# Reordering the first loads and spreading the recurrence's VectorE steps in a kernel that mixes an FFT filter with a state-space recurrence

## The chip, the cores and the metric

The kernel runs on one core of a Trainium2 chip. The metric is the device time of one execution in microseconds (us). Each experiment was timed several times, beside runs of the kernel before on the same chip. A run is called slow when it is over 1.5% above the fastest run of the same kernel; ratios use fast runs only.

Engines: PE is TensorE (matmul; its weight loads are listed as PEld), DVE is VectorE, ACT is ScalarE, POOL is GpSimd, SP is SyncE, which here only issues DMAs. In these traces an instruction that waits holds up those behind it on its engine.

## The reference

With x of 2048 x 1024 in bf16, the output is `g*a + (1-g)*b`:

```python
g = sigmoid((x * gate_w).sum(-1, keepdims=True))
a = irfft2(rfft2(x) * (w_r + 1j*w_i), s=(2048, 1024))     # over both axes
# b: a diagonal complex recurrence over the 2048 rows
Bu = einsum("bld,pd->blp", x, B_bar)
h[t] = Lam_bar * h[t-1] + Bu[t]
b = 2 * einsum("blp,dp->bld", h, Cmat).real + x * Dskip
```

## The kernel before: the parts that matter

The work has three parts.

- **Start**: eight x tiles are loaded, and `fstage` transforms each of them along the rows (product `ps_f` on TensorE).
- **FFT part**: 16 groups `g` run through `fd` (product `ps_d` with the table `G`), `bf_w` (products with `MM`, then VectorE multiplies by the filter `W` into `Y`) and `bi` (`ps_q`); then the inverse transform (`ps_id`, `ps_y`) writes `a` to a scratch in DRAM.
- **Last part**: the gates, then 16 output tiles (product `psy`).

The recurrence runs beside the FFT and the last part. It comes in 16 pairs (4 chunks of rows times 4 pairs of state blocks). A pair is 32 matmuls `psu` of `xT` (x transposed by DMA) with `BT`, four evictions by ScalarE into `u`, and ten large VectorE steps:

```python
def ssm_pair(c, q):
    u = up.tile([P, 2, 2, TC], BF16, name="u", tag="u")
    for jj in range(2):
        for ri in range(2):
            ...                                  # 8 matmuls psu <- BT, xT
            nc.scalar.activation(out=u[:, jj, ri, :], in_=psu, func=ACT.Copy, scale=...)
            if not (jj and ri):
                yield 1.8
    nc.vector.tensor_mul(out=cu, in0=u, in1=...)           # 3 products and sums
    ...
    nc.vector.tensor_tensor_scan(out=su[:, jj, ri, :], ...) # 4 scans
    ...
    nc.vector.tensor_add(out=h, in0=cu, in1=u)             # 3 products and sums
    yield 1.8
```

A `yield` only tells the program, while it is being written out, how much work the generator has emitted; a loop uses it to interleave the recurrence with the FFT. SP and POOL keep the program's order; a scheduler orders the other engines.

The loads of the start:

```python
xts = [load_x(jj) for jj in range(8)]                 # SP's queue
...
for jj in range(8):
    for _ in fstage(jj): pass
    if jj == 5:
        start_consts()      # G_sb, FI_sb    on POOL's queue
        load_M(0)           # MM             on POOL's queue
        load_W(0)           # W              on POOL's queue
    if jj == 4:
        nc.gpsimd.tensor_copy(out=BT[:, 0, 0, 0, 0:1], in_=xts[6][:, 0, 0:1])   # holds BT(0) back until x tile 6 is in
        load_BT(0); load_xT(0); load_BT(1); load_BT(2); load_BT(3)              # transposing DMAs, SP's queue
load_M(1); load_W(1); load_M(2)                       # POOL's queue
```

Of the kernel before, what the change touches and what calls it, by code (L numbers as in the profile page):

```python
# [10 lines left out]
ACT = mybir.ActivationFunctionType  # L11
ALU = mybir.AluOpType
FP32 = mybir.dt.float32
BF16 = mybir.dt.bfloat16
# [6 lines left out]
D = 1024  # L21
K = 512
P = 128
TC = 512
# [101 lines left out]
GN = 2308  # L126
# [10 lines left out]
def kernel(  # L137
# [17 lines left out]
    nc = tc.nc  # L155
# [54 lines left out]
        for ri, src in enumerate((B_B_re, B_B_im)):  # L210
            nc.sync.dma_start_transpose(out=BT[:, jb, ri], in_=src[P * jb:P * (jb + 1), :])

    def load_xT(c):
        for h in range(2):
            r0 = TC * c + 256 * h
            nc.sync.dma_start_transpose(out=xT[:, :, r0:r0 + 256], in_=x[r0:r0 + 256, :])

    xts = [load_x(jj) for jj in range(8)]

    vps = psU.tile([P, 4, 8], BF16, name="vps", tag="psu")  # L220
    for i in range(4):
# [117 lines left out]
        a, s = 4 * (q % 2), TC * (q // 2)  # L339
        return xT[:, a:a + 4, s:s + TC].rearrange("p (j r) t -> p j r t", r=2)  # L340

    def ssm_pair(c, q):
        u = up.tile([P, 2, 2, TC], BF16, name="u", tag="u")
        for jj in range(2):
            jb = 2 * q + jj
            for ri in range(2):
                psu = psU.tile([P, TC], FP32, name="psu", tag="psu")
                for dblk in range(8):
                    nc.tensor.matmul(psu, lhsT=BT[:, jb, ri, dblk, :], rhs=xT[:, dblk, TC * c:TC * (c + 1)],  # L349
                                     start=(dblk == 0), stop=(dblk == 7))  # L350
                nc.scalar.activation(out=u[:, jj, ri, :], in_=psu, func=ACT.Copy,  # L351
                                     scale=(nrho if ri else rho)[:, jb:jb + 1])
                if not (jj and ri):
                    yield 1.8
        tq = tab[:, 2 * q:2 * q + 2]
        full = [P, 2, 2, TC]
        cu = rp.tile(full, BF16, name="cu", tag="cu")
        su = rp.tile(full, BF16, name="su", tag="su")
        nc.vector.tensor_mul(out=cu, in0=u, in1=tq[:, :, 0:1, :].to_broadcast(full))  # L359
        nc.vector.tensor_mul(out=su, in0=u[:, :, ::-1, :], in1=tq[:, :, 1:3, :])  # L360
        nc.vector.tensor_add(out=cu, in0=cu, in1=su)  # L361
        for jj in range(2):
            jb = 2 * q + jj
            for ri in range(2):
                nc.vector.tensor_tensor_scan(out=su[:, jj, ri, :], data0=r_sb[:, jb:jb + 1].to_broadcast([P, TC]),  # L365
                                             data1=cu[:, jj, ri, :],
                                             initial=(0.0 if c == 0 else carry[q][:, jj, ri:ri + 1]),
                                             op0=ALU.mult, op1=ALU.add)
        if c + 1 < NCH:
            ge = su[:, :, :, TC - 1]  # L370
            k1 = sm.tile([P, 2, 2], FP32, name="k1")
            nc.vector.tensor_mul(out=k1, in0=ge, in1=cTC[:, 2 * q:2 * q + 2].unsqueeze(2).to_broadcast([P, 2, 2]))
            k2 = sm.tile([P, 2, 2], FP32, name="k2")
            nc.vector.tensor_mul(out=k2, in0=ge[:, :, ::-1], in1=sg[:, 2 * q:2 * q + 2, :])
            cy = sm.tile([P, 2, 2], FP32, name=f"carry{q}")
            nc.vector.tensor_add(out=cy, in0=k1, in1=k2)
            carry[q] = cy
        h = h_tile(c, q)
        nc.vector.tensor_mul(out=cu, in0=su, in1=tq[:, :, 0:1, ::-1].to_broadcast(full))  # L379
        nc.vector.tensor_mul(out=u, in0=su[:, :, ::-1, :], in1=tq[:, :, 1:3, ::-1])  # L380
        nc.vector.tensor_add(out=h, in0=cu, in1=u)
        hs[c, q] = h
        yield 1.8


    eos = {}
# [1 line left out]
    def fstage(jj):  # L388
# [15 lines left out]
        for eo_i in range(2):  # L404
            for b in range(2):
# [9 lines left out]
                (nc.vector.tensor_copy if eo_i else nc.scalar.copy)(  # L415
                    out=FX[:, q + 1, :, j0:j0 + 4], in_=ps[:, :, 1, :].rearrange("p j c -> p c j"))
                yield 1.0

    gctx = ExitStack()
    gc1 = gctx.enter_context(tc.tile_pool(name="gc1", bufs=1))  # L420
    fr = gctx.enter_context(tc.tile_pool(name="fr", bufs=2))
    G_sb = gc1.tile([P, GN], BF16, name="G_sb")
    FI_sb = fc.tile([P, 2 * P], BF16, name="FI_sb")

    def start_consts():
        nc.gpsimd.dma_start(out=G_sb, in_=cG)
        nc.gpsimd.dma_start(out=FI_sb, in_=cFI)

    MM = {}
    WT = {}  # L430
    Wtiles = [gc1.tile([P, 2, 514], BF16, name=f"W{i}") for i in range(2)]
    for w in Wtiles:
        nc.gpsimd.memset(w[:, :, 513:514], 0.0)
    Xtiles = [gc1.tile([P, 2, 514], BF16, name=f"X{i}") for i in range(2)]
    for w in Xtiles:
        nc.gpsimd.memset(w[:, :, 513:514], 0.0)

    def load_M(g):
        m = fr.tile([P, 6, P], BF16, name="MM", bufs=3)
        (nc.gpsimd if g < 3 else nc.sync).dma_start(out=m, in_=cMM[g])  # L440
        MM[g] = m

    def load_W(g):
        w = Wtiles[g % 2]
        for ri, src in enumerate((A_w_r, A_w_i)):
            rows = bass.AP(src.tensor, src.offset + g * 513, [[32 * 513, 64], [((32 - 2 * g) if g else 16) * 513, 2], [1, 513]])
            nc.gpsimd.dma_start(out=w[:, ri, 0:513], in_=rows)
        WT[g] = w

    X1s, Ys = {}, {}  # L450
    Gi_sb = None
# [147 lines left out]
    def load_C(half):  # L599
# [7 lines left out]

    sp_work = {
        0: [lambda: load_BT(4)], 1: [lambda: load_BT(5)], 2: [lambda: load_BT(6)], 3: [lambda: load_BT(7)],
        5: [lambda: load_xT(1)], 7: [lambda: load_xT(2)], 9: [lambda: load_xT(3)], 11: [lambda: load_C(0)],  # L610
    }

    for jj in range(8):
        for _ in fstage(jj):
            pass
        if jj == 5:
            start_consts()
            load_M(0)
            load_W(0)
        if jj == 4:  # L620
            nc.gpsimd.tensor_copy(out=BT[:, 0, 0, 0, 0:1], in_=xts[6][:, 0, 0:1])
            load_BT(0)
            load_xT(0)
            load_BT(1)
            load_BT(2)
            load_BT(3)
    load_M(1)
    load_W(1)
    load_M(2)

    def ssm_all():
        for c in range(NCH):
            for q in range(4):
                if c == 0:
                    tables(q)
                yield from ssm_pair(c, q)

    class Gen:
        def __init__(self, g):
# [15 lines left out]
    ssm = Gen(ssm_all())  # L655
    fft = Gen(fft_main())
    while not fft.done:
        if ssm.t < 28.8 * (fft.t - 3.5) / (84 - 3.5) and ssm.t < 28.0:
            ssm.step()
        else:  # L660
            fft.step()
    while ssm.t < 28.0:
        ssm.step()
    load_C(1)
    order1.close()
# [2 lines left out]
    with ExitStack() as bctx:  # L668
# [3 lines left out]
        dsk_bc = fin1.tile([P, D], BF16, name="dsk_bc")  # L672
        nc.gpsimd.dma_start(out=dsk_bc, in_=B_Dskip.partition_broadcast(P))

        lrow = fin1.tile([1, 2, D], BF16, name="lrow")
        pc = psY.tile([P, 16], FP32, name="pc", tag="psy")
        gf = fin1.tile([P, 16], FP32, name="gf")
        om = fin1.tile([P, 16], FP32, name="om")

        def gates():  # L680
            for hf in range(2):
                pg = psY.tile([P, D], FP32, name="pg", tag="psy")
                for ch in range(2):
                    t0 = TC * (2 * hf + ch)
                    for dblk in range(8):
                        nc.tensor.matmul(pg[0:1, TC * ch:TC * (ch + 1)], lhsT=gwT[:, dblk:dblk + 1],
                                         rhs=xT[:, dblk, t0:t0 + TC], start=(dblk == 0), stop=(dblk == 7))
                nc.scalar.copy(out=lrow[:, 0, :], in_=pg[0:1, :])
                nc.vector.tensor_sub(out=lrow[:, 1, :], in0=pg[0:1, :], in1=lrow[:, 0, :])
                for tb in range(8):  # L690
                    for i in range(2):
                        nc.tensor.matmul(pc[:, 8 * hf + tb:8 * hf + tb + 1], lhsT=lrow[:, i, P * tb:P * (tb + 1)],
                                         rhs=one, start=(i == 0), stop=(i == 1))
            gb = fin1.tile([P, 16], BF16, name="gb")
            nc.scalar.activation(out=gb, in_=pc, func=ACT.Sigmoid)
            nc.vector.tensor_copy(out=gf, in_=gb)
# [4 lines left out]
        fins = {}  # L701

        def tile_in(tb):
            xc = fin.tile([P, D], BF16, name="xc", bufs=4)
            gac = fin.tile([P, D], BF16, name="gac", bufs=4)
            nc.sync.dma_start(out=xc, in_=x[P * tb:P * (tb + 1), :])
            nc.sync.dma_start(out=gac, in_=ya_dram[P * tb:P * (tb + 1), :])
            nc.vector.tensor_mul(out=xc, in0=xc, in1=dsk_bc)
            nc.scalar.activation(out=gac, in_=gac, func=ACT.Copy, scale=gf[:, tb:tb + 1])  # L709
            fins[tb] = xc, gac  # L710

        psys = {}
# [21 lines left out]
                nc.sync.dma_start(out=out2[P * tb:P * (tb + 1), ds], in_=o[:, ds])  # L734

        def c_all():
            for tb, dh in ((0, 0), (1, 0), (2, 0), (0, 1), (1, 1), (2, 1)):
                if tb + 2 < 5 and dh == 0:
                    tile_in(tb + 1)
                half(tb, dh)  # L740
                yield 3.6
            for tb in range(3, 16):
                if tb + 1 < 16:
                    tile_in(tb + 1)
                half(tb, 0)
                yield 3.6
                half(tb, 1)
                yield 3.6

        while ssm.t < 28.8 + 14.0:  # L750
            ssm.step()
        gates()
        tile_in(0)
        cg = Gen(c_all())
        t0 = ssm.t
        while not cg.done:
# [34 lines left out]
```

## Time and profile before

Time before the change: 387.31 us, median of 3 runs (385.66 to 396.58). The profiled run took 398.2 us (span 396.4 us) and is slow, so it is some 3% longer than the two fast ones (385.66 and 387.31 us).

The first fence holds three rows of the page's busy table of before. Each digit is a fortieth of the span (9.9 us) in tenths of busy time; PEclk is the clock granted to TensorE, in tenths.

```profile
PE   3840889969699598899979999999999999999995
...
DVE  4930345895787499952997799999999999997121
...
PEclk9995799989879899999989999999999999999999
```

Slice 4 (29.7 to 39.6 us) has a 0 for TensorE, and so it has for VectorE. From slice 22 on TensorE is full to the end.

What was waited for, from the waits view of before (engine, line, what ended the wait: total us, times, longest):

```profile
PE psu L349 <- DMA xT<-in_A_x_dram: 17.3, 1, 17.3
...
PE ps_xe L481 <- DMA MM<-c_MM: 8.5, 2, 4.7
...
PE pc L692 <- DVE lrow L689: 2.2, 1, 2.2
```

TensorE waits 17.3 us in one piece for `xT`, 8.5 us for `MM`, and once 2.2 us for the gates' rows (`lrow`). Why is `xT` late? Its two transposing DMAs are issued from 17.6 us on, and the last of them lands at 41.1 us. The next two fences are DMA views of before by queue (q1 is SP's queue, q0 POOL's): first 18 to 38 us, when the copies of POOL's queue (`G`, `FI`, three `MM`, two `W`: 1.7 MB) are in flight, then 41 to 46 us, when they are through.

```profile
q1 hardware_dynamic: 4477, 1.13, 65.4%
q0 software_dynamic: 499, 1.61, 46.0%
```

```profile
q1 hardware_dynamic: 4122, 1.02, 103.8%
```

In the first stretch the transposes move 1.13 MB in 20 us (57 GB/s); in the second 1.02 MB in 5 us (205 GB/s). Their packets are small (1.02 MB in 4122 packets, 250 bytes each), those of the copies large (1.61 MB in 499, 3.2 KB each). The late `xT` moves everything: the first `ps_d` runs at 45.7 us, although the x tiles have landed by about 15. On TensorE the first `psu` runs ahead of the last x tile's `ps_f` and ahead of `ps_d`. From TensorE's timeline of before (start us, us, engine, line, what; in brackets the idle time and what ended it):

```profile
41.24 1.44 PE L349 MATMUL psu<-xT,BT 128*128 128x512 bf16 x3 [17.34 <-DMA xT<-in_A_x_dram]
42.48 0.42 PE L410 MATMUL ps_f<-BT,eo 128*128 128x256 bf16 x1
...
45.66 0.82 PE L458 MATMUL ps_d<-G_sb,big 128*128 128x512 bf16 x5
```

### The profile page before, as it was taken

Reading aid. Unit: us, or ns where it says so; the run is one execution under the profiler, and the core shown is the slowest. Engines: PE = TensorE matmul, PEld = TensorE weight load, DVE = VectorE, ACT = ScalarE, POOL = GpSimd, SP = SyncE. Lnnn points to the kernel's source line nnn. Section 1 sums busy time; section 2 is a strip of 40 time slices with the busy share of each in tenths; the row PEclk is TensorE's granted clock in tenths of the full one; section 3 lists DMA queues with packets and bytes.
Section 4 is the critical chain, followed back from the end, with each engine's and each line's share of the span. In section 5 each row is a group of like instructions: output and inputs, shape, how many; then the busy total and the mean of one; then the engine's idle time right before and its main releaser. Section 6 shows DMA issues by size and latency. Waiting matters only on the chain.

```text
span 396.4 us, 4950 instructions
## 1 busy us (share of the span) xinstructions
PE 346.6 (87%) x1860; PEld 180.9 (46%) x1860; DVE 292.7 (74%) x408; ACT 182.9 (46%) x252; POOL 32.3 (8%) x83
## 2 busy tenths in 40 slices
PE   3840889969699598899979999999999999999995
PEld 2630556635465265564324444444444444444442
DVE  4930345895787499952997799999999999997121
ACT  2960399939677587986325231412322232211100
POOL 4550012202211000000000000000000000000000
PEclk9995799989879899999989999999999999999999
DMA  7799939765969511327950023221121022034001
GB/s 270 233 182 90 166 85 203 209 129 130 179 158 163 122 60 73 141 107 184 187 186 1 2 79 82 78 79 26 55 79 54 27 79 80 2 96 140 30 26 54
DMA packets 65064, 42.91 MB, mean 108 GB/s; under 512 B 52400, under 2 KB 54448, under 8 KB 65040
## 3 DMA queue, kind: packets, MB, share of 16 engines
q1 hardware_dynamic: 62560, 36.12, 38.6%
q0 software_dynamic: 2128, 6.30, 7.0%
q8 instruction: 14, 0.23, 0.3%
q10 hardware_dynamic: 352, 0.17, 0.1%
q14 instruction: 10, 0.08, 0.1%
HBM read 21.61 MB, written 8.39 MB: 76 GB/s over the span
## 4 chain that ended last, share of the span: by engine, by line
PE 58%; DVE 18%; DMA 10%; ACT 7%; SPq 3%; issue 2%; DVEq 0%; POOL 0%; ACTq 0%; POOLq 0%
PE psy L723 28%; PE psu L349 20%; DMA xT<-in_A_x_dram 5%; DVE su L365 5%; DMA xt<-in_A_x_dram 3%; DMA MM<-c_MM 3%; PE ps_d L458 2%; PE psy L726 2%; SPq L603 1%; DVE su L360 1%; DVE cu L379 1%; ACT X L470 1%; DVE cu L359 1%; DVE u L380 1%; ACT X L491 1%
## 5 line engine op out<-in xcount | busy, mean ns | idle before, releaser
L349 PE MATMUL psu<-xT,BT 128*128 128x512 bf16 x512 | 121.5, 383 | 17.4 <-DMA xT<-in_A_x_dram 17.3
L349 PEld LDWEIGHTS <-BT 128*128 128x128 bf16 x512 | 49.7, 98 | 74.9 <-issue 20.4
L365 DVE TENSOR_TENSOR_SCAN su<-r_sb,carry,cu 128x512 bf16<-128x512 f32 x48 | 57.7, 1264 | 0.4
L351 ACT ACTIVATE u<-psu,nrho 128x512 bf16<-128x512 f32 x32 | 22.1, 690 | 60.1 <-PE psu L349 60.1
L723 PEld LDWEIGHTS <-h 128*128 128x128 bf16 x256 | 25.0, 98 | 30.2 <-issue 0.5
L709 ACT ACTIVATE gac<-gac,gf 128x1024 bf16<-128x1024 bf16 x16 | 18.1, 1146 | 39.0 <-DMA gac<-ya_scratch 36.0
L732 DVE SCALAR_TENSOR_TENSOR o<-psy,om,gac 128x1024 bf16<-128x1024 f32 (+1 forms) x17 | 20.6, 1215 | 21.0 <-PE psy L726 21.0
L351 ACT ACTIVATE u<-psu,rho 128x512 bf16<-128x512 f32 x32 | 22.0, 687 | 22.8 <-PE psu L349 22.6
L359 DVE TENSOR_TENSOR cu<-u,tab 128x2048 bf16<-128x2048 bf16 x16 | 19.5, 1219 | 15.3 <-ACT u L351 15.2
L495 DVE TENSOR_TENSOR Y<-X,W 128x1028 bf16<-128x1028 bf16 x16 | 11.1, 693 | 25.8 <-ACT X L491 25.8
L723 PE MATMUL psy<-CT,h 128*128 128x512 bf16 x128 | 29.3, 379 | 0.0
L723 PE MATMUL psy<-big,h 128*128 128x512 bf16 x128 | 28.9, 379 | 0.0
L516 PE MATMUL ps_q<-MM,Y 128*128 128x256 bf16 x64 | 17.2, 298 | 5.3 <-DVE Y L497 3.2
L415 DVE CAST big<-ps_f 128x512 bf16<-128x512 f32 x8 | 5.5, 683 | 21.5 <-ACT big L414 21.5
L458 PE MATMUL ps_d<-G_sb,big 128*128 128x256 bf16 (+3 forms) x128 | 20.5, 300 | 0.0
L379 DVE TENSOR_TENSOR cu<-su,tab 128x2048 bf16<-128x2048 bf16 x16 | 19.5, 1218 | 0.1
L361 DVE TENSOR_TENSOR cu<-cu,su 128x2048 bf16<-128x2048 bf16 x16 | 19.5, 1217 | 0.1
L360 DVE TENSOR_TENSOR su<-u,tab 128x2048 bf16<-128x2048 bf16 x16 | 19.5, 1217 | 0.0
L380 DVE TENSOR_TENSOR u<-su,tab 128x2048 bf16<-128x2048 bf16 x16 | 19.5, 1216 | 0.0
L723 PEld LDWEIGHTS <-xT 128*128 128x128 bf16 x128 | 12.5, 98 | 15.1
L723 PEld LDWEIGHTS <-big 128*128 128x128 bf16 x128 | 12.5, 98 | 15.1
L410 PE MATMUL ps_f<-BT,eo 128*128 128x256 bf16 x64 | 17.6, 311 | 1.7 <-DVE big L415 1.5
(170 smaller groups left out, 579.4 us busy)
## 6 DMA issues: line engine op xcount, KB each, us to landing
ya_scratch<-ya SPq DMA_DIRECT2D x16, 256.0 KB, 2.0
xc<-in_A_x_dram SPq DMA_DIRECT2D x16, 256.0 KB, 2.9
gac<-ya_scratch SPq DMA_DIRECT2D x16, 256.0 KB, 2.9
out_dram<-o SPq DMA_DIRECT2D x15, 256.0 KB, 2.0
MM<-c_MM SPq DMA_DIRECT2D x13, 192.0 KB, 2.6
W<-in_A_w_r_dram POOLq DMA_DIRECT2D x16, 128.2 KB, 4.2
W<-in_A_w_i_dram POOLq DMA_DIRECT2D x16, 128.2 KB, 3.7
xt<-in_A_x_dram SPq DMA_DIRECT2D x4, 512.0 KB, 4.3
```

The source lines that it names most:

```text
L349: nc.tensor.matmul(psu, lhsT=BT[:, jb, ri, dblk, :], rhs=xT[:, dblk, TC * c:TC * (c + 1)], start=(dblk == 0), stop=(dblk == 7))
L351: nc.scalar.activation(out=u[:, jj, ri, :], in_=psu, func=ACT.Copy, scale=(nrho if ri else rho)[:, jb:jb + 1])
L359: nc.vector.tensor_mul(out=cu, in0=u, in1=tq[:, :, 0:1, :].to_broadcast(full))
L360: nc.vector.tensor_mul(out=su, in0=u[:, :, ::-1, :], in1=tq[:, :, 1:3, :])
L361: nc.vector.tensor_add(out=cu, in0=cu, in1=su)
L365: nc.vector.tensor_tensor_scan(out=su[:, jj, ri, :], data0=r_sb[:, jb:jb + 1].to_broadcast([P, TC]), data1=cu[:, jj, ri, :], initial=(0.0 ...
L379: nc.vector.tensor_mul(out=cu, in0=su, in1=tq[:, :, 0:1, ::-1].to_broadcast(full))
L380: nc.vector.tensor_mul(out=u, in0=su[:, :, ::-1, :], in1=tq[:, :, 1:3, ::-1])
L458: nc.tensor.matmul(ps[:, lo:lo + w], lhsT=FX[:, q, 8 * g:8 * g + 8, :], rhs=G_sb[:, o:o + w], start=start, stop=stop, skip_group_check=True)
L709: nc.scalar.activation(out=gac, in_=gac, func=ACT.Copy, scale=gf[:, tb:tb + 1])
L723: nc.tensor.matmul(psy[:, ds], lhsT=hs[c, jb // 2][:, jb % 2, ri, P * tq:P * (tq + 1)], rhs=CT[dh][:, jb, ri, :], start=(i == 0), stop=False)
L732: nc.vector.scalar_tensor_tensor(out=o[:, ds], in0=psy[:, ds], scalar=om[:, tb:tb + 1], in1=gac[:, ds], op0=ALU.mult, op1=ALU.add)
```

## The change

Its intent: bring in everything that the first FFT groups need, then run the transposes with nothing beside them; break up the transposes inside the FFT; and emit the ten VectorE steps of a pair one at a time among the FFT's steps, so that no FFT step waits behind a whole pair. The diff, cut to its core:

```diff
-    xts = [load_x(jj) for jj in range(8)]
+    xts = [load_x(jj) for jj in range(5)]
+    nc.sync.dma_start(out=G_sb, in_=cG)
+    xts.append(load_x(5))
+    load_M(0)
+    xts.append(load_x(6))
+    load_W(0)
+    xts.append(load_x(7))
+    load_M(1); load_W(1); load_M(2)            # all on SP's queue now
+    nc.sync.dma_start(out=FI_sb, in_=cFI)
...                                             # and the BT(0) hold waits for x tile 7
-        5: [load_xT(1)], 7: [load_xT(2)], 9: [load_xT(3)], 11: [load_C(0)],
+        13: [load_C(0)],
+    for i in range(6):
+        sp_work[5 + i] = [load_xT(1 + i // 2, (i % 2,))]     # one half per group
...
-    def ssm_pair(c, q):           # TensorE, ScalarE and all VectorE steps
+    def ssm_pe(c, q, u):          # TensorE and ScalarE, a yield after each eviction
+    def ssm_dve(c, q, u):         # a yield after each of ten VectorE steps
...
+                for i, _ in enumerate(ssm_pe(c, q, u)):
+                    yield 0.5
+                    for _ in range(2 + i % 2):
+                        next(prev, None)         # steps of the pair before
+                        yield 0.52
+                prev = ssm_dve(c, q, u)
...
-        if ssm.t < 28.8 * (fft.t - 3.5) / (84 - 3.5) and ssm.t < 28.0:
+        if ssm.t < 28.8 * (fft.t - 3.5) / (88 - 3.5) and ssm.t < 30:
...
-        while ssm.t < 28.8 + 14.0:              # how far the recurrence is when the gates come
+        while ssm.t < 41:
...                                             # last part, in words:
-    gates(): row sums, their transposing products `pc`, sigmoid, all before the first output tile
+    gates(): row sums only;  gates2(): the rest, after the second half tile
+    scaling gac by the gate: ScalarE, just before a tile's second half
+    tiles are loaded two ahead instead of one
```

So the VectorE steps of a pair now stand beside the matmuls of the next pair, one pair later than before. No arithmetic is added or taken away.

## The prediction

> **What bounds the kernel now.** The profiled run (396.4 us, flagged slow; timed runs 385.7 to 396.6) has three parts.
>
> 1. *Start, to 45.7 us.* The timeline shows TensorE idle from 24.0 to 41.2 us; the waits view charges 17.3 us of it to the DMA of xT. Two transposing loads each of xT and BT (1.5 MB) are issued from 14.9 us; xT lands at 41.1. While POOL's copies (G, FI, three MM, two W: 1.7 MB) are in flight, the DMA view shows mostly 60 to 210 GB/s; after them the next transposes run at about 290. So the transposes are starved, which fits the Trainium skill ("DMA: Bandwidth & Descriptors", section "Queues, rings and completion order"): each DMA engine round-robins between queues packet by packet, and transposes have small packets. The first product of G (ps_d) runs only at 45.7 us, though the x tiles are in by about 15.
> 2. *FFT with four recurrence pairs, 45.7 to 183 us.* TensorE 87%, ScalarE 82%, VectorE 72% busy: none is the limit; in-order queues make them wait. The chain of waits shows 6.9 and 3.1 us for MM behind transposes in SP's queue, 5.9 us of SP issuing CT's transposes ahead of the last MM, and VectorE recurrence steps (four scans, 4.5 us) ahead of Y and pm.
> 3. *After that.* TensorE is 100% busy from 206 us on, VectorE 95% until 362. A pair takes 14.24 us of TensorE, about 13.7 of VectorE.
>
> **What the change does.**
> - Start: about 1 MB goes ahead of the last x tile: at 380 GB/s (seen there) +3 us on x, but only 0.7 MB, in the same queue, still competes with the transposes. Estimate: transposes from 18.5 us, xT landed by 28 to 30. G, MM and W are there when the last x tile is transformed (about 25 us), so ps_d starts at about 27, not 45.7.
> - FFT phase: xT in six single transposes, CT after the last MM: about -10 us of MM stalls. VectorE steps come one by one, about 3.2 instead of 4 pairs of them (11.9 us each) in this phase: -3 to -8 us. Phase about 124 instead of 137 us.
> - After: gates come after 5.7 pairs instead of 6, their transposing products later: -5 us before the first output tile, but +3 us of recurrence left, and VectorE one pair behind. From the FFT's end TensorE needs about 213 us, VectorE 210 (12.8 pairs, 12 tiles at 1.8, a 31 us tail): no gain; VectorE may become co-limiting.
>
> No arithmetic is added or removed.
>
> **Sum.** 27 + 124 + 213 = about 365 us. What start and FFT phase save is nearly all critical, since everything else comes after. What the slow flag means is unknown: if before's fast runs lost less in the start, the gain is smaller than against the profile. Predicted 365 us, 80% range 353 to 378. Faster by over 2%: 0.88; within 2%: 0.10; slower: 0.02.
>
> **What would show it.** First ps_d at 25 to 30 us; psu's wait for xT down from 17.3 to under 5 us; no 10 us gap with every engine idle; MM waits under 3 us in all; FFT end (last ps_y) near 150 us; from there about 213 us, TensorE full, VectorE over 95%.
>
> **What would make it wrong.** psu placed ahead of ps_d on TensorE, still waiting for xT; x tiles delayed by more than 3 us; W loads, still on POOL's queue, starving the later transposes; VectorE, a pair behind, costing the last part 5 to 15 us; the granted clock (0.5 in some stretches) moving.

## The result

The changed kernel took 370.1 us (median of 4 runs, 367.28 to 370.15). Before, with one more run, had 391.94 us (385.66 to 397.66). The ratio is 0.953 (95% interval 0.9445 to 0.9616); a ratio here is the mean time of one kernel's fast runs over that of the other's fast runs of the same rounds, so it is not quite the ratio of the medians. On another chip (the run changed_again) it was 0.9418. The change is faster by 4.7% and 5.8% on these two.

The same views of the changed kernel, profiled with a span of 368.3 us. The busy table, in slices of 9.2 us:

```profile
PE   3978899999987999999959999999999999999995
...
DVE  4958358997999643994987999999999999997221
...
PEclk9999999999998999999998999999999999999999
```

The hole at the start is gone. From the waits view:

```profile
ACT gac L757 <- DVE gf L713: 9.9, 1, 9.9
...
PE psu L382 <- ACT u L384: 5.0, 2, 4.7
DVE xc L725 <- DMA gac<-ya_scratch: 4.9, 1, 4.9
...
PE psu L382 <- DMA xT<-in_A_x_dram: 1.1, 1, 1.1
```

The wait for `xT` fell from 17.3 to 1.1 us, and no wait of TensorE for `MM` is left in the list. But there are new ones: ScalarE waits 9.9 us for `gf`, and TensorE 4.7 us in one piece for ScalarE. The DMA view of the changed kernel from 19 to 35 us, where the first transposes run, shows no packet of POOL's queue (q0); q1 moved its 2.91 MB at 182 GB/s:

```profile
q1 hardware_dynamic: 11530, 2.91, 107.3%
```

On TensorE `ps_d` now stands ahead of the first `psu`:

```profile
27.64 0.82 PE L469 MATMUL ps_d<-G_sb,big 128*128 128x512 bf16 x5
29.60 0.38 PE L382 MATMUL psu<-xT,BT 128*128 128x512 bf16 x1 [1.14 <-DMA xT<-in_A_x_dram]
```

Three marks in time, read from the timelines, divide the span (us; the third column is the changed kernel on the second chip):

| | before (slow run) | changed | changed_again |
|---|---|---|---|
| first `ps_d` | 45.7 | 27.6 | 27.7 |
| end of the last `ps_y` | 180.1 | 149.4 | 147.2 |
| FFT part, the difference | 134.4 | 121.8 | 119.5 |
| from there to the end of the span | 216.3 | 218.9 | 220.2 |

(The prediction put the end of before's FFT part at 183 us, where the loads of the last part begin; by the measure of this table it is 180.1.) The start gained 18 us, the FFT part 12.6, and the last part lost 2.6. Part of the difference to the slow run is its state.

**The clock is part of it.** The next fence shows the five stretches of before where TensorE had work at half clock. Columns: stretch, its us, busy us of PE, PEld, DVE, ACT and POOL with instruction counts, PEclk, DMA share, GB/s.

```profile
41.20:45.60 4.40, 4.36 (x19) 2.63 (x20) 0.56 (x1) 0.58 (x1) 0.00 (x0) 0.52 1.02 203
86.30:89.80 3.50, 3.49 (x16) 2.35 (x17) 3.50 (x5) 1.01 (x1) 0.57 (x1) 0.51 0.00 0
106.80:113.70 6.90, 5.88 (x24) 3.22 (x25) 6.39 (x11) 2.25 (x4) 1.71 (x3) 0.51 1.09 243
134.10:137.60 3.50, 3.50 (x18) 2.15 (x16) 1.01 (x2) 2.51 (x4) 0.00 (x0) 0.51 0.00 0
202.40:205.80 3.40, 3.40 (x11) 0.89 (x9) 3.40 (x4) 1.00 (x1) 0.00 (x0) 0.50 0.31 114
```

Together they last 21.7 us, so with the clock at half they cost at most half of that, 10.9 us (an estimate). They come just after TensorE stood still: for `xT` until 41.2, for `Y` until 86.3, for `MM` until 107.8 and 134.0, for the gates until 201.9. The Trainium skill has a rule for this ("TensorE: Matmul & The Clock Gate", Part 1, the clock gate): after an idle window of about 3.4 us the clock is halved, and a busy window of about 3.4 us brings it back. On the length of the slow stretches this trace agrees: four of them last about 3.4 or 6.9 us, and in the fifth only the end of a longer one had work. On the idle window it does not: the stalls before them lasted 17.3, 3.0, 3.7, 4.7 and 2.2 us, so that two were shorter than 3.4 us. The changed kernel has two stretches, both after a stall (the first after a wait of 2.6 us for the inverse table `Gi_sb`; the stall before the second is the middle line):

```profile
114.80:118.20 3.40, 3.40 (x17) 2.44 (x15) 2.70 (x3) 2.50 (x3) 0.00 (x0) 0.50 0.01 2
188.90:193.30 4.40, 0.33 (x2) 0.05 (x1) 3.44 (x7) 1.14 (x2) 0.00 (x0) 1.00 0.00 0
193.30:196.70 3.40, 2.77 (x7) 0.99 (x7) 1.17 (x2) 3.40 (x6) 0.00 (x0) 0.50 0.02 5
```

They last 6.8 us, at most 3.4 us lost. So up to some 7 of the 28 us between the two profiles (an estimate, the difference of these two) are clock that stalls no longer take away; they are part of the gains by stage above, not a further gain. The mean granted clock, 0.957 before, is 0.989 now. It also goes with the spread from run to run: of the 7 runs of before on one chip, the fastest (389.55 us) had 0.973 and the slowest (401.09 us) 0.950.

### The profile page after: what moved, and what is told of

The parts are those of the page before. It is cut to its first block, busy times and chain, and to the rows that moved or that the text cites. A ratio compares the mean times of both kernels' runs of the same rounds, so it can differ in the third digit from the quotient of the medians.

```text
span 368.3 us, 4955 instructions
## 1 busy us (share of the span) xinstructions
PE 340.3 (92%) x1860; PEld 178.9 (49%) x1860; DVE 294.0 (80%) x408; ACT 180.0 (49%) x252; POOL 28.3 (8%) x74
## 4 chain that ended last, share of the span: by engine, by line
PE 57%; issue 17%; DMA 9%; DVE 6%; POOL 5%; SPq 4%; ACT 0%; ACTq 0%; DVEq 0%; POOLq 0%
PE psy L739 27%; PE psu L382 20%; PE ps_id L538 5%; POOL W L239 4%; SPq L614 3%; DMA CT<-in_A_x_dram 2%; DMA W<-in_A_w_i_dram 2%; PE psy L742 2%; DMA Gi_sb<-c_Gi 1%; DVE su L402 1%; DMA vec<-in_B_Lambda_im_dram 1%; PE ps_y L560 1%; DMA gac<-ya_scratch 1%; PE ps_y L559 1%; PE ps_y L558 1%
## 5 line engine op out<-in xcount | busy, mean ns | idle before, releaser
L384 ACT ACTIVATE u<-psu,rho 128x512 bf16<-128x512 f32 x32 | 22.2, 695 | 41.7 <-PE psu L382 32.1
L384 ACT ACTIVATE u<-psu,nrho 128x512 bf16<-128x512 f32 x32 | 22.2, 692 | 14.5 <-PE psu L382 14.3
L538 PE MATMUL ps_id<-Gi_sb,big 128*128 128x256 bf16 (+3 forms) x128 | 18.8, 304 | 2.6 <-DMA Gi_sb<-c_Gi 2.6
L527 PE MATMUL ps_q<-MM,Y 128*128 128x256 bf16 x64 | 15.4, 274 | 5.4 <-DVE Y L508 2.8
L739 PEld LDWEIGHTS <-big 128*128 128x128 bf16 x128 | 12.5, 98 | 15.1
L739 PEld LDWEIGHTS <-xT 128*128 128x128 bf16 x128 | 12.5, 98 | 15.1
L452 PE MATMUL ps_f<-BT,eo 128*128 128x256 bf16 x64 | 16.8, 302 | 3.1 <-ACT big L457 1.7
L538 PEld LDWEIGHTS <-big 128*128 128x128 bf16 x128 | 15.9, 148 | 6.4 <-issue 3.3
```

Source lines behind the costliest of these rows:

```text
L538: nc.tensor.matmul(ps[:, lo:lo + w], lhsT=FX[:, q, :, j], rhs=Gi_sb[:, o:o + w], start=start, stop=stop, skip_group_check=True)
L739: nc.tensor.matmul(psy[:, ds], lhsT=hs[c, jb // 2][:, jb % 2, ri, P * tq:P * (tq + 1)], rhs=CT[dh][:, jb, ri, :], start=(i == 0), stop=False)
```

## The experiments

Theory 1: the start carries most of the gain, because the transposes are freed of the copies in the other queue. Theory 2: spreading the VectorE steps carries it. Twelve kernels ran; all gave correct results. Kernels are compared below by the means of their fast runs where they ran on one chip; where they did not, the text says so.

### One part alone, or all but one (one chip)

**start_only**: before, with only the new start.

```diff
 # before
+    G, MM(0), W(0) between the x tiles; MM(1), W(1), MM(2), FI behind them; SP's queue; BT(0) held for x tile 7
```

> The kernel before with only the start changed (tables, W and G between the x tiles on SP's queue, transposes after the last x tile). Theory 1 (the start carries most of the gain): first ps_d near 28 us instead of 45.7, xT wait of psu about 1 us, time 10 to 18 us under before, about 370 to 377 us. Theory 2 (the spread of VectorE's steps carries it): less than 6 us under before, because VectorE stays the limit later on.

Measured: 373.99 us, ratio 0.9539 (0.9468 to 0.9611). First `ps_d` at 28.4 us.

**no_start**: the changed kernel with before's start.

```diff
 # changed
-    G, MM, W, FI early on SP's queue
+    G, MM, W, FI after fstage(5) on POOL's queue; BT(0) held for x tile 6
```

> The changed kernel with the start put back as it was (tables on POOL's queue, beside the transposes). Theory 1: first ps_d back near 40 to 46 us, time 10 to 18 us above the changed kernel, about 380 to 388. Theory 2: under 376 us.

Measured: 382.01 us, ratio 0.9757 (0.9682 to 0.9831). First `ps_d` at 45.0 us, and `psu` waits 16.7 us for `xT`.

**spread_only**: before, with the new emission of VectorE's steps and its constants.

```diff
 # before
-    ssm_pair; 84, 28.0
+    ssm_pe and ssm_dve, one step at a time; 88, 30
```

> The kernel before with only the VectorE steps spread (and the mixing constants that go with it, gates where before has them). Theory 1: 0 to 6 us under before's fast runs, 381 to 388 us. Theory 2: 8 us or more under before, below 379.

Measured: 392.52 us, ratio 1.0032 (0.9952 to 1.0111): nothing (before itself took 392.55 us on this chip, more than the absolute numbers above assumed). In its profile (span 390.0 us) the FFT part takes 123.4 us (42.5 to 166.0), 11 less than in the slow profile of before, but 224.0 us remain after it, 8 more than in before. The reason stands in its waits view:

```profile
PE pc L709 <- DVE lrow L706: 8.4, 1, 8.4
```

VectorE, now a pair behind, makes `lrow` late, and the gates' products, still in their old place, hold TensorE for 8.4 us. The changed kernel moves them to a later place (`gates2`).

**no_spread**: the changed kernel with before's emission.

```diff
 # changed
-    ssm_pe and ssm_dve; 88, 30, 41
+    ssm_pair; 84, 28.0, 28.8 + 14.0
```

> The changed kernel with the recurrence's VectorE steps emitted pair by pair as before and before's mixing constants and gate position; start, SP order and end stay changed. Theory 1: within 6 us of the changed kernel, 367 to 376 us. Theory 2: 376 us or more.

Measured: 369.21 us, ratio 0.9425 (0.9362 to 0.9488). That is as fast as the changed kernel (0.953 and 0.9418 on two other chips).

What follows: theory 1 holds. The start alone gives 4.6%; without it 2.4% are left. The spread gives nothing measurable, neither alone nor as the last part added. But it is not idle: its FFT part ends at 149.4 us in the changed kernel and at 154.5 in no_spread, whose last part is shorter (212.9 us against 218.9). What the spread gains in the FFT part is lost afterwards. Where, the last two groups show.

### The order on SP's queue (second chip, with the next two)

**changed_again**: the changed kernel unaltered, for comparison.

> The changed kernel itself, for comparison on one chip. Both theories: 367 to 371 us, 0.94 to 0.955 of before.

Measured: 368.73 us, ratio 0.9418 (0.9287 to 0.9549).

**no_spwork**: the changed kernel with before's transposes inside the FFT.

```diff
 # changed
-    one half of xT at each of groups 5 to 10, CT at 13
+    a whole xT at groups 5, 7 and 9, CT at 11
```

> The changed kernel with the transposes inside the FFT put back (xT by pairs at four groups, CT ahead of the last MM). If the MM waits behind transposes cost what the chain of waits of before showed (some 10 us): 4 to 10 us above the changed kernel, MM waits of 5 us or more. If they only moved slack: within 2 us of it.

Measured: 374.31 us, ratio 0.9601 (0.9507 to 0.9695). The means of the fast runs are 374.1 against 367.7 us for changed_again: 6.4 us (5.3 if changed_again's run of 372.24 us, which counts as slow, is taken in). `MM` waits are back, 5.0 us of them in one piece:

```profile
PE ps_xe L492 <- DMA MM<-c_MM: 5.5, 2, 5.0
```

So `MM` loads that queue behind transposes are a real cost, of the predicted kind.

### What starves the transposes

Four placements of the same 1.7 MB are compared: in POOL's queue while the transposes run (no_start), and the three below.

**early_pool**: as early as in the changed kernel, but on POOL's queue.

```diff
-    nc.sync.dma_start(out=G_sb, in_=cG)          # and FI, MM(0..2), W(0..1)
+    nc.gpsimd.dma_start(out=G_sb, in_=cG)        # at the same place in the program
```

> The changed kernel with tables, W and G issued just as early but on POOL's queue. If what matters is that they are through before the transposes start: within 4 us of the changed kernel, xT landing within 31 us. If POOL's queue itself is the trouble: 8 us or more above it.

Measured: 374.9 us, ratio 0.9615 (0.9541 to 0.9689): 6.9 us above changed_again by the means of the fast runs (374.6 and 367.7), between the two numbers that the theories named, so this run decides neither as written. Its profile does say what happened. The transposes are not starved: `xT` is in at 34.9 us, 10.6 us after the first BT transpose was issued (24.25); in changed_again these are 29.5, 18.6 and 10.9. The x tiles pay instead: SP's last four take 11.8 us to land (median) against 7.8 in the changed kernel, because all of POOL's copies now share the engines with them from the first microseconds on.

**late_sp**: on SP's queue, behind the first transposes.

```diff
+            load_BT(0)
+            load_xT(0)
+            G, MM(0), W(0), MM(1), W(1), MM(2), FI     # SP's queue
             load_BT(1)
```

> The changed kernel with tables, W and G on SP's queue but behind the first transposes of BT and xT (all after the x tiles). If the starving comes from two queues sharing the engines packet by packet, one queue in order must spare the transposes: xT lands by 26 us, psu waits under 4 us for it, time 0 to 6 us above the changed kernel because G comes later. If any 1.7 MB in flight beside them starves the transposes: xT lands after 33 us and the time is 8 us or more above.

Measured: 368.55 us, ratio 0.9429 (0.9317 to 0.9541), the same as the changed kernel (fast means 367.4 and 367.7 us). So being ahead of the transposes is not what matters. `xT` was in at 26.7 us, just after the 26 expected. (Its profiled run is a slow one; only the start is read from it.)

**mid_sp** (third chip): on SP's queue, in the very place where before had them in flight.

```diff
             load_BT(0)
+            G, MM(0), W(0), MM(1), W(1), MM(2), FI     # SP's queue
             load_xT(0)
```

> The changed kernel with the same 1.7 MB (tables, W, G) on SP's queue in the very place where before's POOL queue had them in flight: between the first BT transposes and those of xT. If only the sharing of engines between two queues starves the transposes, xT lands later than in late_sp (26.7 us) by about what 1.7 MB take at 380 GB/s, 4 to 6 us: 31 to 33 us, and the time is 2 to 8 us above the changed kernel. If the bytes in that place are the trouble whatever the queue, xT lands near before's 38 to 41 us.

Measured: 373.89 us, ratio 0.9541 (0.9438 to 0.9645). `xT` landed at 34.2 us, a little later than the expected 31 to 33. The first `ps_d` did not wait for it: on TensorE it stood ahead of `psu` here and ran at 26.7 us. The time was lost later, in an FFT part of 129.7 us with a wait of 4.8 us for `MM`. So a late `xT` holds the FFT's start only where `psu` stands in front; whether before could be mended by moving its first `psu` back on TensorE alone was not tried. The three timelines show the first `psu`, which is what `xT` releases: no_start, late_sp and mid_sp in this order (start us, us, engine, line, what; in brackets the idle time and what ended it).

```profile
40.35 0.58 PE L348 MATMUL psu<-xT,BT 128*128 128x512 bf16 x1 [16.66 <-DMA xT<-in_A_x_dram]
```

```profile
26.67 1.01 PE L372 MATMUL psu<-xT,BT 128*128 128x512 bf16 x2 [2.71 <-DMA xT<-in_A_x_dram]
```

```profile
34.25 1.89 PE L372 MATMUL psu<-xT,BT 128*128 128x512 bf16 x7 [2.05 <-DMA xT<-in_A_x_dram]
```

With nothing in front, `xT` is there at 26.7 us. With 1.7 MB in front in the same queue it is there 7.5 us later, of which 2.0 are only a later issue of the first transpose (17.1 against 15.1 us). With the same 1.7 MB at about the same time in another queue it is 13.7 us later. (The three ran on three chips; the changed kernel's own `xT` came at 29.6 and 29.5 us on two, while before's start gave 38.4 us in spread_only, 40.35 in no_start and 41.2 in before.) The Trainium skill ("DMA: Bandwidth & Descriptors", section "Queues, rings and completion order") says that each DMA engine takes turns between its queues packet by packet. A queue of 250-byte packets that takes turns with one of 3.2 KB packets would lose, which agrees with the extra 6 us of no_start over mid_sp, but is not shown by it: the other queue is also the only one that the view calls software_dynamic, and no run put the copies on a second hardware queue. The other half of the delay goes with the bytes in front. Turns do not explain everything: from 34 to 38 us in before the DMA view has only 51 copy packets (39.8% of the engines' time) and still no more than 391 of the transposes, against 2970 in the 4 us from 42. And late_sp has such a stretch with nothing in any other queue: 134 packets of the transposes, at 17 GB/s, from 22.2 to 24.2 us. So such a stretch does not need another queue; what causes it stays open, and part of the extra 6 us may be of this kind.

### The new wait of the last part (third chip)

In the changed kernel the gates' last step puts `gf` on VectorE, behind a recurrence pair (the end of it, from VectorE's timeline):

```profile
183.36 4.81 DVE L402 TENSOR_TENSOR_SCAN su<-r_sb,carry,cu 128x512 bf16<-128x512 f32 x4
...
190.82 1.22 DVE L423 TENSOR_TENSOR big<-cu,u 128x2048 bf16<-128x2048 bf16 x1
191.96 0.17 DVE L713 CAST gf<-gb 128x16 f32<-128x16 bf16 x1
```

ScalarE then stands before a `gac` scaling that needs `gf`, and the evictions `u` behind it hold up TensorE. The timeline of ScalarE in the changed kernel:

```profile
182.04 0.18 ACT L712 ACTIVATE gb<-pc 128x16 bf16<-128x16 f32 x1 [0.70 <-PE pc L709]
192.16 1.15 ACT L757 ACTIVATE gac<-gac,gf 128x1024 bf16<-128x1024 bf16 x1 [9.94 <-DVE gf L713]
193.22 0.67 ACT L384 ACTIVATE u<-psu,rho 128x512 bf16<-128x512 f32 x1
```

The sigmoid is done at 182.2 us, `gf` comes 9.9 us later, and the next eviction runs at 193.2. TensorE stands still from 189.2 to 193.9 us and then runs at half clock.

**gate_off_dve**:

```diff
-            nc.vector.tensor_copy(out=gf, in_=gb)
+            nc.scalar.copy(out=gf, in_=gb)
-            nc.vector.tensor_scalar(out=ob, in0=gb, ...); nc.vector.tensor_copy(out=om, in_=ob)
+            nc.gpsimd.tensor_scalar(out=ob, in0=gb, ...); nc.gpsimd.tensor_copy(out=om, in_=ob)
```

> The changed kernel with the three small copies after the sigmoid taken off VectorE (gf to ScalarE, om to POOL), so that the gac scaling doesn't wait for 10 us behind a recurrence pair. If this new wait costs what TensorE's 4.7 us stall shows: 3 to 5 us under the changed kernel, 363 to 366 us. If VectorE, a pair behind, limits the end anyway: within 1.5 us of it.

Measured: 362.93 us, ratio 0.9261 (0.9149 to 0.9373): 5 to 7 us under the changed kernel's fast means on two other chips (367.7 and 369.4), and the fastest kernel (one of its four runs, 369.24 us at a clock of 0.990, counts as slow and is left out). The changed kernel itself did not run on this chip. The same place in its timeline, and its clock:

```profile
180.26 0.18 ACT L712 ACTIVATE gb<-pc 128x16 bf16<-128x16 f32 x1 [2.56 <-PE pc L709]
180.47 0.20 ACT L713 CAST gf<-gb 128x16 f32<-128x16 bf16 x1
...
182.09 0.69 ACT L384 ACTIVATE u<-psu,rho 128x512 bf16<-128x512 f32 x1 [0.23 <-PE psu L382]
```

```profile
core 0: 360.3 us, clock 1.000
```

`gf` follows the sigmoid at once, no stall is left there, and the granted clock is full throughout the profiled run. From the last `ps_y` to the end it takes 212.7 us instead of 218.9.

**gate_and_tiles**: the same, and the first two x tiles of the last part loaded ahead of CT's transposes.

```diff
+            if tb == 1:
+                load_C(1)        # after the first two xc loads instead of before them
```

> The same, and the first two x tiles of the last part loaded before the transposes of CT, so that VectorE doesn't idle 4.9 us for them. If both stalls are real and critical: 6 to 9 us under the changed kernel, 360 to 363 us. If TensorE is the limit of the end: no better than gate_off_dve.

Measured: 363.82 us, ratio 0.9299 (0.9184 to 0.9414): no better than gate_off_dve, so the second half of the guess was wrong. VectorE's idle time for these tiles, 4.9 us in the changed kernel, was not critical there; gate_off_dve itself shows only 2.0 us of it.

**no_spread_fixed_end**: no_spread with both repairs.

> no_spread with the same two repairs of the end. If the spread saves about 7 us in the FFT phase and gives it back in the stalls of the end, the repaired end makes the spread pay: this kernel 3 us or more above gate_and_tiles. If the spread only moves VectorE work from one part to the other: within 2 us of gate_and_tiles.

Measured: 369.29 us, ratio 0.9428 (0.9338 to 0.9518). By the means of the fast runs that is 369.2 against 363.8 us for gate_and_tiles on the same chip: the spread is worth 5.4 us once the end is repaired. FFT parts end at 155.7 and 148.3 us, and what follows takes 212.2 and 212.7. So the spread's gain in the FFT part was real, and the wait for `gf` hid it. (no_spread's ScalarE waits 6.5 us for `gf` too, but its TensorE then loses only 1.2 us to `u`, against 5.0 in the changed kernel; the repair gains it nothing.) Not run was the changed kernel with only its end put back.

## Why the prediction was right

The time came out at 370.1 us, 5 us above the 365 predicted and inside the range; the main cause of the gain was the one named, the starved `xT`. Some of the closeness is luck: against the span, start, FFT part and last part came out 0.6 us over, 2.2 under and 5.9 over, so that the second hid a part of the third. Point by point:

- **Start: right.** Predicted: transposes from 18.5 us, `xT` in by 28 to 30, first `ps_d` at 27. The trace: 18.6, 29.6 and 27.6. Undone alone (no_start) it takes away half of the gain or more; alone (start_only) it gives 4.6%. The reason was half the story: mid_sp puts about half of `xT`'s delay down to the bytes ahead of it, and the rest goes with the other queue. That `G` is there early, which the prediction counted on too, is not what freed `ps_d`: it was there by 25.3 us in before, and late_sp, which issues it at 24.45 us, is as fast. What held `ps_d` was the `psu` in front of it on TensorE, which the prediction named only as a risk for the new kernel.
- **FFT part: right in size.** 124 us predicted, 121.8 measured. "About -10 us of MM stalls" was 6.4 us by experiment. "-3 to -8 us" for the spread fits what the repaired end shows, 5.4 us.
- **Last part: the term that was mis-sized.** Predicted 213 us "no gain"; it took 218.9. The risk that VectorE, "a pair behind", might cost "the last part 5 to 15 us" was named but not counted. It came, not as a lack of VectorE throughput, but as a chain of in-order waits: VectorE's pair, `gf`, `gac`, `u`, TensorE. With it gone the part takes 212.7 us, the number that was predicted.
- **The clock: not costed.** It was listed as something that might move. It moved in favour, by at most some 7 us between the two profiles, as a consequence of the stalls that went away.
- **Of the signs named**, the wait for `xT` (1.1 us), the `MM` waits (none), the hole at the start (gone) and the end of the FFT (149.4 us against "near 150") came as said. "TensorE full" afterwards did not, between 189.2 and 193.9 us. VectorE, for which over 95% was named, was busy for 95% of the time from the last `ps_y` to 334 us (175.0 of 184.6 us).

## What to carry to other kernels

Before transposing DMAs on which everything waits, look at what other queues have in flight: here the same bytes in the same queue, in order, cost about half as much delay, and just behind the transposes they cost no time that the runs could show (367.4 against 367.7 us). Look too at what stands behind the waiting instruction on its engine. When one engine's work is set back in order to smooth another part, search for small steps on that engine that a third engine waits for, and move them to an engine that is free: here three tiny steps, the first of them `gf`, hid the gain of the spread. Count a stall of TensorE of several us with the half-clock time that follows it.

## What the Trainium skill lacked or had wrong

- "DMA: Bandwidth & Descriptors" describes the turns between queues, but gives no number for a transposing DMA beside plain copies of another queue. Here the transposes fell from 205 to 57 GB/s, and `xT` came 13.7 us later with 1.7 MB in another queue, against 7.5 with them in its own.
- The same page does not explain the stretch of before (34 to 38 us) in which transposes crawled (391 packets in 4 us, against 2970) beside as few as 51 copy packets, nor the one of late_sp (134 packets in 2 us) with no other queue at work.
- "TensorE: Matmul & The Clock Gate", Part 1, has the clock halved after an idle window of about 3.4 us. Here stalls of 2.2, 2.6 and 3.0 us were followed by half clock as well, while one of 2.4 us in gate_off_dve (clock 1.000) was not. The slow stretches themselves, about 3.4 and 6.9 us, agree with it.
- Its remark in Part 1 that, for modelling, the ramp costs under 1% of a typical span is about a kernel's warm-up and must not be carried to one that stalls several times: here five stalls left 21.7 us of work at half clock, at most 10.9 us or 2.7% of the span of before.
